# Two of 64 row maxima of a unit taken over by ScalarE, GpSimd and a short VectorE reduction

## The chip, the cores and the metric

The kernel runs on one core of one Trainium2 chip. The metric is the device time of one execution in microseconds (us); the time of record is the median of a few runs. TensorE (PE in the profile, PEld for its weight loads), VectorE (DVE), ScalarE (ACT), GpSimd (POOL) and SyncE (SP, which issues nearly all DMAs) each work through their own instructions in order and wait for each other by semaphores.

## What is computed

Two attention blocks share one input of 2048 tokens by 512, and a gate mixes their outputs. Cut to what matters here:

```python
x = A_x
g = sigmoid((x * gate_w).sum(-1, keepdims=True))
# A: 32 heads of 16, every query sees all 2048 keys
p = softmax(einsum("bhqd,bhkd->bhqk", q, k) * scale, axis=-1)
a = einsum("bhqk,bhkd->bhqd", p, v) ... @ A_wo
# B: 32 heads, four segments of 512 tokens; within a segment causal softmax,
# plus a memory term from the segments before
for s in range(4):
    p = softmax(einsum(qs, ks) * scale + mask)
    o = g_h * (pq @ M) / (pq @ z + 1e-6) + (1 - g_h) * (p @ vs)
    M, z = M + pk.T @ vs, z + pk.sum()
b = o ... @ B_wo
out = g * a + (1 - g) * b
```

The maximum of every row of scores is needed before the exponentials. The kernel gets it with a first pass of score products, on the orientation that has the queries on the partitions, and folds it into the second pass, on the transposed orientation, as two extra rows of q.

## The kernel before

A first stage (until about 300 us) computes q, k, v and the memory, and begins with the maxima. Then the main stage runs over 2368 slots. A unit is a side (A or B), four heads and one chunk of 512 queries; an A unit has 64 slots, a B unit 10, and they alternate, so 74 slots make a pair of units.

In slot n, three things are issued. The score product (`score_product`, L1064) puts a 128x512 tile `st` into one of three PSUM banks and ScalarE takes its exponential to `p` in SBUF (L1083). The max product (L242), for the slot that is `LEAD` = 96 slots ahead, puts a 128x512 tile into one of four PSUM banks `sm`, and VectorE reduces it to one column of `pm` (`max_part`, L275: a TENSOR_REDUCE over 512 columns). About every seventh max slot belongs to side B; there VectorE runs up to two masked reductions (L290). The score and the max product of a slot use different halves of TensorE's rows.

After every third slot (`BURST` = 3) comes a run of P @ V (`some_values`, L155): pieces of 128 queries of four heads, usually three or four pieces. `most(n)` sets how many; `MOST` = 3 is the short run. All P @ V of a unit accumulate in the one bank `ops`; when the unit is done ScalarE copies `ops` to `oraw` (L1137) and SP stores it.

Twelve slots in every pair of units are a stretch of their own (`unit_end`): no P @ V runs there, and 24 half products of the output projection (or of a later q tile) go through the same bank `ops`, between the score and max products of the twelve slots. It begins right after, or within a few slots after, the last P @ V of an A unit. The P @ V of the B unit follows it: its pieces come from three `p` tiles, the first read by the first run after the stretch, the second by the second half of the second run.

GpSimd serves four things in one queue. (1) The diagonal tiles of B's `p` are masked by AFFINE_SELECT (L1092, `score_values`): one select for the first tile, then three together, two for the second tile and one for the third. P @ V of a tile waits for its select. (2) When a unit's last maximum is there, `finish_max` (L214 to L224) joins the columns of `pm`; TensorE transposes them and a DMA places them in the q tile. (3) An octet of heads that is done is normalised (`octet`): the factors, with a power (L1200) first, and later the scaling of the 128x512 tile `v` (L1216), for B the memory's share `vM` added (L1218), then the two halves `hl` (L1224, L1225), which SP stores. (4) Halves of weights (L948, L949) and the sum of two output parts (L1307). `at(n, f)` puts an action into the program when slot n is reached; within the twelve-slot stretch such actions come between its steps.

Of the kernel before, what the change touches and what calls it, by code (L numbers as in the profile page):

```python
# [10 lines left out]
F32 = mybir.dt.float32  # L11
F32R = mybir.dt.float32r
AF = mybir.ActivationFunctionType
ALU = mybir.AluOpType
AX = mybir.AxisListType
# [7 lines left out]
CH = 512  # L23
# [11 lines left out]
LEAD = 96  # L35
BURST = 3
LATER = (2, 3)
MOST = 3
# [9 lines left out]
def gated_mix(ctx, tc, x, xT, wqkv, a_wo, b_wq, b_wk, b_wv, b_wo, beta, gate_w, out):  # L48
    nc = tc.nc
# [67 lines left out]
    maxs = []  # L117
    for k in range(NU):
        mine = {u: iter(range(32)) for u in range(2)}
# [13 lines left out]
    last_max = {u: m for m, (u, _) in enumerate(maxs)}  # L133
# [23 lines left out]
    def wait_early(n, count=BURST):  # L157

        loads_ = []
        for m in range(n + 1 + LEAD, n + 1 + count + LEAD):  # L160
            if m < nS:
                u, (r, i) = maxs[m]
                loads_ += lands.pop(("q", u, r), []) + lands.pop(("k", u, r, u[2] if u[0] == "B" else i // 8), [])
        for u, j in slots[n + 1:n + 1 + count]:
            for r in range(2):
                loads_ += lands.pop(("score", u, r), [])
        for x in loads_:
            tc.add_manual_dep(behind[0].ins, x.ins.name, mybir.DependencyInfo(
                mybir.DependencyClass.Sync, mybir.DependencyReason.DATA), reason="loads of the next burst")
# [71 lines left out]
    def max_product(ps, u, h, s, n0, n, k, k0=0):  # L241
        nc.tensor.matmul(ps[:, n0:n0 + n], rows(qt[u][:, :, s * 128:(s + 1) * 128], h, 48), rows(k[:, :, k0:k0 + n], h, 48),  # L242
                         start=True, stop=True)
# [3 lines left out]
    def flush_rows():  # L247
        while rows_left:
            rows_left.pop(0)()
# [3 lines left out]
    def oldest():  # L253

        return min(read_last, key=read_last.get)

    def was_read(b):

        if b is not None:
            read_last[b] = count[0] = count[0] + 1  # L260
    count = [4]

    def max_part(m, bank, b=None):

        u, (r, i) = maxs[m]
        side, g, c = u
        if u not in pmt:
            pmt[u] = mp.tile([128, 4, 4] + [4] * (side == "A"), F32, tag="pm" + side, name="pm")
        pm = pmt[u]
        ps = bank()  # L270
        if side == "A":

            kc, s, h = i // 8, i % 8 // 2, 2 * r + i % 2
            max_product(ps, u, h, s, 0, CH, kt_[u, kc])
            nc.vector.tensor_reduce(pm[:, h, s, kc:kc + 1], ps, axis=AX.X, op=ALU.max, negate=True)  # L275
            was_read(b)
            flush_rows()
        else:


            k = kt_[u, c]
            if b is not None:
                read_last[b] = 9 * nS
            mine = [(2 * r + h, s, 128 * (s == 2) + 256 * (s == 1 and h), 128 * (s + 1))
                    for h, s in (((0, 0), (0, 2)), ((0, 1), (1, 1)), ((1, 0), (1, 2)), ((0, 3),), ((1, 3),))[i]]
            for h, s, n0, w in mine:
                max_product(ps, u, h, s, n0, w, k)
            flush_rows()
            def masked(h, s, n0, w):
                nc.vector.tensor_tensor_reduce(  # L290
                    out=tri["rest"][:, 0:w], in0=ps[:, n0:n0 + w], in1=tri["mask"][:, CH - w:], scale=-1.0, scalar=3.0e38,
                    op0=ALU.add, op1=ALU.min, accum_out=pm[:, h, s:s + 1])
                was_read(b)

            for h, s, n0, w in mine:
                rows_left.append(lambda h=h, s=s, n0=n0, w=w: masked(h, s, n0, w))
            rows_left.pop(0)()
        if m == last_max[u]:
            def finish():

                due = min(e for e in a_last if e >= last_max[u]) + LATE_T
                late.append((min(due, first[u] + LEAD - 12), u, finish_max(u)))
            todo.append((m + 1, finish))
# [616 lines left out]
    fr = ctx.enter_context(tc.tile_pool(name="fr", bufs=1, reuse_waits="tile"))  # L920
# [4 lines left out]
    banks = [sm_ps.tile([128, CH], F32, name=f"sm{i}") for i in range(4)]  # L925
# [111 lines left out]
    wide = range(nS - LEAD + 2, nS - 4)  # L1037
# [6 lines left out]
    queue = []  # L1044
# [121 lines left out]
    def at(n, f):  # L1166
        beside.setdefault(n, []).append(f)
# [188 lines left out]
    def most(n):  # L1356

        if not queue:
            return 0
        _, u, done = queue[0]  # L1360
        side, left = u[0], SLOTS[u[0]] - done
        runs = (first[u] + SLOTS[side] + GAP[side] + 1 - n) // BURST
        if side == "B" or runs < 1:
            return ends[side].get(left, MOST + (len(queue) > LOW))
        due = min(SLOTS[side], (n + BURST - GAP[side] - first[u] + 1) // 4 * 4) - done
        return MOST + (left - 4 >= (MOST + 0.5) * runs and (due > 2 * MOST or runs == 1))
# [1 line left out]
    filled = [0]  # L1368
    turns = [0]

    def maximum(n):

        b = oldest()
        max_part(n + LEAD, lambda: banks[b], b)

    def unit_end(n0):

# [49 lines left out]
    n = 0  # L1427
    while n < nS or queue or beside or filled[0] < len(fill):
        for f in beside.pop(n, []):
            f()  # L1430
        if shared and n % BURST == 0:
            n += END - 1
            unit_end(n - END + 1)
            for x in range(n - END + 1, n + 1):
                for f in beside.pop(x, []):
                    f()
            wait_early(n)
            n += 1
            continue
        if n < nS:  # L1440
            score_tile(n)
            score_product(n)
            score_values(n)
        m = n + LEAD
        if m < nS:
            loads(m + PRE)
            maximum(n)
        run_todo(m)
        if n >= nS or n % (2 * BURST if n in wide else BURST) == (2 * BURST if n in wide else BURST) - 1:
            taken = some_values(n, 8 if n >= nS or n in wide else most(n))  # L1450
            if n < 5:


                for i in range(4):
                    nc.tensor.matmul(ops[:, 128 * i:128 * i + 128], identf, identf, start=True, stop=True)
            if any(e[0] < m + 1 for e in late):
                run_late(st_ps, "st", m + 1)
            else:

                for _ in range(0 if n >= nS and queue else 4 if n not in wide else 11 - taken if taken < 8 else 0):  # L1460
                    if filled[0] == len(fill) or fill[filled[0]][0] > n:
                        break
                    fill[filled[0]][1]()
                    filled[0] += 1
            if 5 < n < nS:
                wait_early(n)
        n += 1
# [3 lines left out]
    for b in range(4):  # L1471
# [3 lines left out]
        t = fr.tile([128, D], F32, tag="v" if b % 2 else "res", name="res", bufs=2)  # L1475
# [37 lines left out]
```

## Time and profile before

| what | value |
|---|---|
| median of 3 runs | 1750.01 us (1749.66 to 1750.13) |
| profiled execution, own time | 1750.37 us |
| its span in the trace | 1748.7 us |
| granted TensorE clock | 1.000 |
| busy, of the span: PE | 1730.6 us (99%) |
| DVE | 1599.5 us (91%) |
| ACT | 1439.9 us (82%) |
| POOL | 735.6 us (42%) |
| DMA | 261.67 MB, mean 150 GB/s |

The span runs from the first to the last recorded instruction; 1.7 us of the execution lie outside it. A row of a group gives the instructions' summed busy time, the mean of one, and the idle time of the engine just before them with what ended it. Records of neighbouring instructions overlap, so the step from one start to the next says more of an engine's rate than the mean length does. The ends of matmuls are modelled, so starts are used for TensorE as well.

### The profile page before, as it was taken

Reading aid. Unit: us, or ns where it says so; the run is one execution under the profiler, and the core shown is the slowest. Engines: PE = TensorE matmul, PEld = TensorE weight load, DVE = VectorE, ACT = ScalarE, POOL = GpSimd, SP = SyncE. Lnnn points to the kernel's source line nnn. Section 1 sums busy time; section 2 is a strip of 40 time slices with the busy share of each in tenths; the row PEclk is TensorE's granted clock in tenths of the full one; section 3 lists DMA queues with packets and bytes.
Section 4 is the critical chain, followed back from the end, with each engine's and each line's share of the span. In section 5 each row is a group of like instructions: output and inputs, shape, how many; then the busy total and the mean of one; then the engine's idle time right before and its main releaser. Section 6 shows DMA issues by size and latency. Waiting matters only on the chain.

```text
span 1748.7 us, 42288 instructions
## 1 busy us (share of the span) xinstructions
PE 1730.6 (99%) x15565; PEld 922.6 (53%) x15565; DVE 1599.5 (91%) x3327; ACT 1439.9 (82%) x2763; POOL 735.6 (42%) x992
## 2 busy tenths in 40 slices
PE   9999999999999999999999999999999999999999
PEld 7887775544444455444444444445444445444445
DVE  7757788999999999999999999999999999999931
ACT  6545557898888898888888888888888888888884
POOL 3543233234352427443435253535344353435442
PEclk9999999999999999999999999999999999999999
DMA  6786567335443446454545454455445444544542
GB/s 207 259 287 218 197 226 213 116 100 147 123 150 106 138 121 182 127 148 124 142 132 147 121 149 124 133 145 127 143 130 148 128 131 118 150 118 145 149 152 63
DMA packets 149390, 261.67 MB, mean 150 GB/s; under 512 B 39064, under 2 KB 61624, under 8 KB 148672
## 3 DMA queue, kind: packets, MB, share of 16 engines
q1 hardware_dynamic: 146640, 254.42, 48.8%
q0 software_dynamic: 2400, 4.29, 0.9%
q8 instruction: 124, 2.03, 0.5%
q14 instruction: 82, 0.67, 0.1%
q10 hardware_dynamic: 144, 0.26, 0.1%
HBM read 174.39 MB, written 83.25 MB: 147 GB/s over the span
## 4 chain that ended last, share of the span: by engine, by line
PE 97%; ACT 2%; issue 0%; DMA 0%; DVE 0%; POOL 0%
PE ops L155 39%; PE st L1064 27%; PE sm L242 14%; PE pr L366 9%; PE pair L366 4%; PE sm L155 2%; ACT p L1083 1%; PE mt_ps L232 0%; PE tps L831 0%; PE sm L1064 0%; DMA vs<-wqkv 0%; PE mps L845 0%; ACT res L1305 0%; PE num L804 0%; PE den L808 0%
## 5 line engine op out<-in xcount | busy, mean ns | idle before, releaser
L1083 ACT ACTIVATE p<-st 128x512 f32<-128x512 f32 x2261 | 1196.2, 603 | 150.2 <-PE sm L242 97.8
L275 DVE TENSOR_REDUCE pm<-sm 128x1 f32<-128x512 f32 x2048 | 1279.7, 683 | 11.2 <-PE sm L242 8.8
L242 PE MATMUL sm<-kA,qA 48*128 48x512 f32 x2048 | 688.3, 428 | 0.1
L1064 PE MATMUL st<-qA,kA 50*128 50x512 f32 x2014 | 676.9, 430 | 7.7 <-ACT p L1083 7.2
L1064 PEld LDWEIGHTS st<-qA,kA 50*128 50x128 f32 x2014 | 332.1, 185 | 419.1 <-ACT p L1083 382.5
L155 PE MATMUL ops<-p,vA 128*17 128x256 f32 (+3 forms) x6360 | 552.2, 445 | 0.0
L242 PEld LDWEIGHTS sm<-kA,qA 48*128 48x128 f32 x2048 | 339.8, 185 | 14.6 <-DVE ph L449 3.9
L1200 POOL TENSOR_TENSOR rcp<-rec,minus 128x32 f32<-128x32 f32 x43 | 234.8, 5461 | 89.3 <-DMA rec<-dend 85.0
L290 DVE CUSTOM_DVE_ANT_0 rest<-sm,mask 128x128 f32<-128x128 f32 (+3 forms) x512 | 246.8, 482 | 0.2
L155 PEld LDWEIGHTS ops<-p,vA 128*17 128x17 f32 x6360 | 129.3, 96 | 214.3 <-issue 183.7
L1092 POOL TENSOR_SCALAR_AFFINE_SELECT p<-p 128x512 f32<-128x512 f32 x128 | 78.6, 637 | 289.9 <-ACT p L1083 288.5
L242 PE MATMUL sm<-kB,qB 48*128 48x128 f32 (+3 forms) x512 | 162.7, 378 | 0.0
L1064 PE MATMUL st<-qB,kB 50*128 50x512 f32 (+2 forms) x495 | 114.2, 329 | 0.3 <-ACT mt L235 0.3
L1064 PEld LDWEIGHTS st<-qB,kB 50*128 50x128 f32 x495 | 77.7, 186 | 47.2 <-ACT p L1083 35.2
L155 PE MATMUL ops<-p,vB 128*17 128x128 f32 (+3 forms) x1504 | 87.5, 350 | 0.0
L155 PE MATMUL ops<-wA,blk 64*128 64x512 f32 x264 | 78.9, 405 | 3.1
L242 PEld LDWEIGHTS sm<-kB,qB 48*128 48x128 f32 x512 | 80.3, 185 | 0.2
L214 POOL TENSOR_TENSOR dm<-pm 128x32 f32<-128x32 f32 x32 | 7.9, 247 | 170.0 <-DVE pm L275 170.0
L155 PE MATMUL ops<-wB,blk 64*128 64x512 f32 x264 | 75.5, 392 | 0.0
L437 POOL TENSOR_SCALAR mn<-full 128x512 f32<-128x512 f32 x24 | 37.0, 1540 | 76.9 <-ACT full L432 76.9
L223 POOL CAST ms<-pm 128x16 fp32r<-128x16 f32 x32 | 6.3, 197 | 136.4 <-DVE pm L290 136.4
L155 PEld LDWEIGHTS ops<-wA,blk 64*128 64x128 f32 x264 | 45.5, 185 | 14.8 <-issue 11.6
(319 smaller groups left out, 1752.3 us busy)
## 6 DMA issues: line engine op xcount, KB each, us to landing
kA<-kdA SPq DMA_DIRECT2D x256, 128.0 KB
vA<-vdA SPq DMA_DIRECT2D x31, 544.0 KB
kA<-kdA SPq DMA_DIRECT2D x256, 64.0 KB
qB<-qdB SPq DMA_DIRECT2D x192, 64.0 KB
kB<-kdB SPq DMA_DIRECT2D x192, 64.0 KB
kdA<-q SPq DMA_DIRECT2D x32, 256.0 KB
qdB<-q SPq DMA_DIRECT2D x32, 256.0 KB
qA<-qdA SPq DMA_DIRECT2D x64, 128.0 KB
```

The source lines that it names most:

```text
L155: behind[0] = nc.tensor.matmul(*args, **kw)
L214: nc.gpsimd.tensor_sub(dm, pm[:, :, :, 2:4], pm[:, :, :, 0:2])
L223: nc.gpsimd.tensor_copy(ms[:, :, 0], nv)
L242: nc.tensor.matmul(ps[:, n0:n0 + n], rows(qt[u][:, :, s * 128:(s + 1) * 128], h, 48), rows(k[:, :, k0:k0 + n], h, 48), start=True, stop=True)
L275: nc.vector.tensor_reduce(pm[:, h, s, kc:kc + 1], ps, axis=AX.X, op=ALU.max, negate=True)
L290: nc.vector.tensor_tensor_reduce(out=tri["rest"][:, 0:w], in0=ps[:, n0:n0 + w], in1=tri["mask"][:, CH - w:], scale=-1.0, scalar=3.0e38, op ...
L366: nc.tensor.matmul(ps, l, r, start=start, stop=stop)
L437: nc.gpsimd.tensor_scalar_min(ph["mn"], full, 0.0)
L1064: nc.tensor.matmul(ps[:, n0:n0 + CH - q0], rows(k[:, :, b * 128:(b + 1) * 128], h, 50), rows(q[:, :, q0:], h, 50), start=True, stop=True)
L1083: nc.scalar.activation(p[:, h], ps, AF.Exp, scale=SCALE)
L1092: nc.gpsimd.affine_select(out=x, in_=x, pattern=[[0, 4], [1, 128]], base=0, channel_multiplier=-1, compare_op=ALU.is_ge, fill=0.0)
L1200: eng.tensor_tensor(r, rec, minus, op=ALU.pow)
```

## The change

In `maximum`, for the last slot of a burst, the length of the P @ V run that follows is looked at. If it is over three pieces, and the max slot belongs to an A unit with more than 40 max slots left, and the unit has given away fewer than two (`SHARE`) and none in the last 20 slots (`SPACE`), then VectorE doesn't reduce the bank. ScalarE copies the 128x512 bank to SBUF (`halves`). Two, four and six slots later GpSimd halves it to 256, 128 and 64 columns; a halving is three instructions, a difference, a clamp and a sum, which together make the larger of two values. Thirty-four slots after the copy VectorE reduces the 64 columns that are left. Slots of `unit_end` and of the last 96 slots never do this. In this program 50 of 2048 A maxima are moved, the first at slot 59 and the last at slot 2213, one or two a unit.

```diff
-    def max_part(m, bank, b=None):
+    def max_part(m, bank, b=None, copied=None):
...
-            nc.vector.tensor_reduce(pm[:, h, s, kc:kc + 1], ps, axis=AX.X, op=ALU.max, negate=True)
+            if copied:
+                copied(ps, pm[:, h, s, kc:kc + 1])
+            else:
+                nc.vector.tensor_reduce(pm[:, h, s, kc:kc + 1], ps, axis=AX.X, op=ALU.max, negate=True)
...
-    def maximum(n):
+    SHARE, SPACE = 2, 20
+    taken_by = {}
+
+    def by_halves(n):
+
+        def copied(ps, pm):
+            t = fr.tile([128, CH], F32, tag="halves", name="halves", bufs=2)
+            nc.scalar.copy(t, ps)
+
+            x = fr.tile([128, CH // 2], F32, tag="above", name="above", bufs=1)
+
+            def halve(w):
+                nc.gpsimd.tensor_sub(x[:, 0:w], t[:, 0:w], t[:, w:2 * w])
+                nc.gpsimd.tensor_scalar(x[:, 0:w], x[:, 0:w], 3.0e38, 0.0, op0=ALU.min, op1=ALU.max)
+                nc.gpsimd.tensor_add(t[:, 0:w], t[:, w:2 * w], x[:, 0:w])
+            for i, w in enumerate((256, 128, 64)):
+                at(n + 2 + 2 * i, lambda w=w: halve(w))
+            at(n + 34, lambda: nc.vector.tensor_reduce(pm, t[:, 0:64], axis=AX.X, op=ALU.max, negate=True))
+        return copied
+
+    def maximum(n, run=0):
 
         b = oldest()
-        max_part(n + LEAD, lambda: banks[b], b)
+        u = maxs[n + LEAD][0]
+        mine = taken_by.setdefault(u, [])
+        yes = (run > MOST and u[0] == "A" and len(mine) < SHARE and last_max[u] - n - LEAD > 40
+               and not (mine and n - mine[-1] < SPACE))
+        if yes:
+            mine.append(n)
+        max_part(n + LEAD, lambda: banks[b], b, by_halves(n) if yes else None)
+
+    def next_run(n):
+
+        return min(most(n), sum(e[0] <= n and e[1] == queue[0][1] for e in queue)) if queue else 0
...
-            maximum(n)
+            maximum(n, next_run(n) if n % BURST == BURST - 1 and n not in wide else 0)
```

TensorE's and SP's instructions stand in the same order before and after. Three places show what moves elsewhere; line numbers differ by 3 or 33 between the two programs.

On GpSimd, the twelve-slot stretch that begins at slot 1104 (about 957 us in the trace of before). `p` is the tile that the select masks for P @ V, `v`, `vM` and `hl` are the scaling of an octet. Before, from the first select to the three selects for the second and third tile:

```order
L1092 AFFINE_SELECT p<-p 128x4x128
L1216 TENSOR_TENSOR v<-v,inv 128x512
L1218 TENSOR_TENSOR v<-v,vM 128x512
L1224 CAST hl<-v 128x4x128
L1225 TENSOR_TENSOR hl<-v,hl 128x4x128
L1092 AFFINE_SELECT p<-p 128x4x128 x3
```

And now, from the third instruction of the first halving on (the first select and the other two of that halving stand directly ahead of it):

```order
L1388 TENSOR_TENSOR halves<-halves,above 128x256
L1386 TENSOR_TENSOR above<-halves 128x128
L1387 TENSOR_SCALAR above<-above 128x128
L1388 TENSOR_TENSOR halves<-halves,above 128x128
L1386 TENSOR_TENSOR above<-halves 128x64
L1387 TENSOR_SCALAR above<-above 128x64
L1388 TENSOR_TENSOR halves<-halves,above 128x64
L1219 TENSOR_TENSOR v<-v,inv 128x512
L1221 TENSOR_TENSOR v<-v,vM 128x512
L1227 CAST hl<-v 128x4x128
L1228 TENSOR_TENSOR hl<-v,hl 128x4x128
L1095 AFFINE_SELECT p<-p 128x4x128 x3
```

The nine instructions of slot 1103's maximum now stand between the first select and the scaling, and so ahead of the three selects.

On the same engine, the stretch that begins at slot 1251 (about 1047 us), where two moved maxima, those of slots 1226 and 1247, come close together. Before, from the last factor of an octet on:

```order
L1206 TENSOR_TENSOR rec<-rec,gB_3261 128x32
L1092 AFFINE_SELECT p<-p 128x4x128
L1216 TENSOR_TENSOR v<-v,inv 128x512
L1218 TENSOR_TENSOR v<-v,vM 128x512
L1224 CAST hl<-v 128x4x128
L1225 TENSOR_TENSOR hl<-v,hl 128x4x128
L1092 AFFINE_SELECT p<-p 128x4x128 x3
```

Now, from the last three instructions of slot 1247's second halving on; ahead of them, behind the factor, stand the nine of slot 1226 and the three of slot 1247's first halving:

```order
L1386 TENSOR_TENSOR above<-halves 128x128
L1387 TENSOR_SCALAR above<-above 128x128
L1388 TENSOR_TENSOR halves<-halves,above 128x128
L1095 AFFINE_SELECT p<-p 128x4x128
L1386 TENSOR_TENSOR above<-halves 128x64
L1387 TENSOR_SCALAR above<-above 128x64
L1388 TENSOR_TENSOR halves<-halves,above 128x64
L1219 TENSOR_TENSOR v<-v,inv 128x512
L1221 TENSOR_TENSOR v<-v,vM 128x512
L1227 CAST hl<-v 128x4x128
L1228 TENSOR_TENSOR hl<-v,hl 128x4x128
L1095 AFFINE_SELECT p<-p 128x4x128 x3
```

Fifteen instructions now stand between the factor and the first select, and three more between that select and the scaling.

On ScalarE, the end of the A unit at slot 881 (about 820 us). `p<-st` are exponentials, `oraw<-ops` empties the bank that the stretch at slot 882 uses next. Before:

```order
L235 CAST mt<-mt_ps 64x128
L1083 ACTIVATE p<-st 128x512 x15
L1137 COPY oraw<-ops 128x512
L1083 ACTIVATE p<-st 128x512 x3
L1080 ACTIVATE p<-st 128x2x256
```

Now:

```order
L235 CAST mt<-mt_ps 64x128
L1086 ACTIVATE p<-st 128x512 x15
L1381 COPY halves<-sm_3294 128x512
L1140 COPY oraw<-ops 128x512
L1086 ACTIVATE p<-st 128x512 x3
L1083 ACTIVATE p<-st 128x2x256
```

The copy of a maximum stands directly ahead of the copy of `ops`, with no exponential between them.

## The prediction

> **What bounds the kernel now.** I read the window of the main stage first, then the timeline of TensorE and VectorE inside it, then the waits. The columns of the first row are the window, its length, and busy time with instruction counts of PE, PEld, DVE, ACT and POOL.
>
> ```profile
> 320.00:1660.00 1340.00, 1328.16 (x12905) 645.80 (x12905) 1337.42 (x2851) 1195.48 (x2308) 574.17 (x784) 1.00 0.47 134
> ```
>
> Two engines look full: VectorE with 1337 of 1340 us and TensorE with 1328. Which of them waits for the other decides what 50 removed reductions are worth. Two stretches of VectorE and one of TensorE say it.
>
> ```profile
> 802.60 7.86 DVE L275 TENSOR_REDUCE pm<-sm 128x1 f32<-128x512 f32 x13
> ...
> 842.59 7.62 DVE L275 TENSOR_REDUCE pm<-sm 128x1 f32<-128x512 f32 x12
> ```
>
> ```profile
> 803.47 0.84 PE L155 MATMUL ops<-p,vA 128*17 128x384 f32 x8
> 804.24 0.50 PE L1064 MATMUL st<-qA,kA 50*128 50x512 f32 x1
> ...
> 805.17 1.05 PE L155 MATMUL ops<-p,vA 128*17 128x512 f32 x8
> 806.15 0.50 PE L1064 MATMUL st<-qA,kA 50*128 50x512 f32 x1
> ```
>
> A reduction is 0.683 long. The first stretch steps (7.86 - 0.68)/12 = 0.598 us, the second (7.62 - 0.68)/11 = 0.631. So 0.598 is VectorE's own rate, three of them 1.79 us a burst, and in the second stretch it loses 0.1 us a burst although no idle shows. TensorE's burst with a run of four pieces is 804.24 to 806.15 = 1.91 us, 0.93 for the products and 805.17 to 806.15 = 0.98 for the run; a run of three takes 803.47 to 804.24 = 0.77, which makes 1.70. Where runs are of four, TensorE is the slower one and VectorE waits for it. TensorE in its turn hardly waits for VectorE:
>
> ```profile
> PEld sm L242 <- DVE pm L275: 0.3, 2, 0.2
> PEld ops L155 <- POOL p L1092: 1.2, 5, 0.2
> ```
>
> The columns are us in total, times and longest. That list counts idle weight loads alone, so I looked for places where a product starts just when its bank is released. One is the end of a twelve-slot stretch:
>
> ```profile
> 918.24 0.69 DVE L275 TENSOR_REDUCE pm<-sm 128x1 f32<-128x512 f32 x1
> ...
> 918.65 0.18 PEld L1064 LDWEIGHTS st<-qA,kA 50*128 50x128 f32 x1 [0.34 <-ACT p L1083]
> ...
> 918.98 0.18 PEld L242 LDWEIGHTS sm<-kA,qA 48*128 48x128 f32 x1
> ```
>
> The max product should start with the score product at 918.65 and starts at 918.98, 0.05 after the reduction ends at 918.93: 0.33 us lost to VectorE. In short: TensorE sets the pace, VectorE trails by one or two per cent, and what delays TensorE, from whichever engine, goes into the time in full.
>
> **VectorE, removed and added.** Removed are 50 x 0.598 = 29.9 us. Added are 50 reductions of 64 columns from SBUF, which no row shows. The nearest are the masked reductions, here with a 384- and a 128-column tile:
>
> ```profile
> L290 DVE CUSTOM_DVE_ANT_0 rest<-sm,mask 128x384 f32<-128x384 f32 x120 | 65.7, 548 | 0.0
> ...
> L290 DVE CUSTOM_DVE_ANT_0 rest<-sm,mask 128x128 f32<-128x128 f32 x120 | 33.8, 281 | 0.1
> ```
>
> The slope is (548 - 281)/256 = 1.04 ns a column, so 0.598 - 448 x 0.00104 = 0.13 us; the bounds are 0.07 (the slope alone) and 0.28. I take 0.13. VectorE is relieved by 50 x 0.47 = 23.4 us, but only what lasts until a place like 918.98 reaches TensorE. The relief is lost wherever VectorE waits for TensorE before that, as in the stretch of fours. Ahead of 918.98 one maximum is taken at slot 1025, four bursts before; I count 0.2 us of the 0.33 as won there, since the short reduction of an earlier maximum comes back in between, and five such places among the 50: -1.0 us, with -7 as the far end (0.46 us at fifteen places).
>
> **ScalarE, added.** Each copy is like the copy of `ops`, which steps 821.42 - 820.94 = 0.48 us:
>
> ```profile
> 820.94 0.59 ACT L1137 COPY oraw<-ops 128x512 f32<-128x512 f32 x1
> ...
> 821.42 1.09 ACT L1083 ACTIVATE p<-st 128x512 f32<-128x512 f32 x2
> ```
>
> Fifty make 24 us. In a burst of 1.91 us the three exponentials take some 1.45 (three of about 0.48), so the copy ends near the moment the next exponential is due, and three score banks cover the rest. That cover is missing where the copy stands directly ahead of `oraw` (slot 881): the last exponential ends just before 820.94 now, so `oraw` starts 0.4 later, and so does the first half product, which needs the emptied bank and follows `oraw` closely now. Ten takes stand so. In five the stretch ends at a place like 918.98, where TensorE then arrives later and loses less to VectorE; I count these at nothing and the other five at 0.4 each: +2.0 us (0 to 4).
>
> **GpSimd, added.** Nine instructions a maximum. Their prices come from these groups (x count | busy, mean ns | idle before):
>
> ```profile
> L1216 POOL TENSOR_TENSOR v<-v,inv 128x512 f32<-128x512 f32 x31 | 39.8, 1284 | 26.0 <-DMA inv<-rdA 19.7 <-DMA inv<-rdB 4.9 <-DMA qB<-qdB 1.3
> L437 POOL TENSOR_SCALAR mn<-full 128x512 f32<-128x512 f32 x24 | 37.0, 1540 | 76.9 <-ACT full L432 76.9
> ...
> L1224 POOL CAST hl<-v 128x512 fp32r<-128x512 f32 x31 | 18.9, 610 | 2.0
> ```
>
> ```profile
> 805.75 0.24 POOL L214 TENSOR_TENSOR dm<-pm 128x32 f32<-128x32 f32 x1 [7.43 <-DVE pm L275]
> 806.07 0.31 POOL L215 TENSOR_SCALAR dm<-dm 128x32 f32<-128x32 f32 x1
> ```
>
> Between 32 and 512 columns a two-input operation costs 0.24 to 1.28 us, so 0.73, 0.45 and 0.31 at 256, 128 and 64; a one-input operation, by L215 and L437, 0.31 to 1.54, so 0.88, 0.56 and 0.39. That is 2 x 1.49 + 1.83 = 4.8. Between dependent instructions lies 806.07 - 805.75 - 0.24 = 0.08, nine times 0.7: 5.5 us a maximum, 275 us in all. If the clamp ran at the rate of the CAST (0.61 at 512) it would be 4.8; with two operations in the clamp, and no row for minimum and maximum together, twice the clamp is the other bound, 7.3. [...]
>
> GpSimd is 43% busy and most of its work has microseconds to spare: the copies at slots 857, 935 and 1004 find it idle, and VectorE's short reduction comes 34 slots later. What matters is what stands behind the nine. In the stretch at slot 1104 that is an octet's scaling and then the selects for P @ V of side B:
>
> ```profile
> 956.88 0.65 POOL L1092 TENSOR_SCALAR_AFFINE_SELECT p<-p 128x512 f32<-128x512 f32 x1 [5.56 <-ACT p L1083]
> 957.59 1.28 POOL L1216 TENSOR_TENSOR v<-v,inv 128x512 f32<-128x512 f32 x1
> ...
> 962.25 1.80 POOL L1092 TENSOR_SCALAR_AFFINE_SELECT p<-p 128x512 f32<-128x512 f32 x3
> ```
>
> ```profile
> 966.63 0.84 PE L155 MATMUL ops<-p,vB 128*17 128x128 f32 x16
> ```
>
> The second half of the run at 966.63 needs the second tile's first select. A run grows by 0.98 - 0.77 = 0.21 us a piece, so that half starts at about 966.87. Before, the select was done at 962.25 + 0.64 = 962.9, 4 us early. Now: free at 957.5, nine instructions until 963.0, scaling 962.25 - 957.59 = 4.66 until 967.7, select until 968.3, and the wait takes 0.05: 1.5 us late. TensorE stands in order, so everything behind the piece waits too. Four takes are like this one (slots 659, 1103, 1547, 1991; a fifth, 215, has a shorter scaling behind it and just about fits): +6.0 us.
>
> In the stretch at slot 1251 two maxima are queued:
>
> ```profile
> 1041.90 0.25 POOL L1206 TENSOR_TENSOR rec<-rec,gB 128x32 f32<-128x32 f32 x1
> ...
> 1053.44 1.81 POOL L1092 TENSOR_SCALAR_AFFINE_SELECT p<-p 128x512 f32<-128x512 f32 x3
> ```
>
> ```profile
> 1057.22 0.84 PE L155 MATMUL ops<-p,vB 128*17 128x128 f32 x16
> ```
>
> From 1042.2: two maxima 11.0 and the first select 0.65, so the scaling starts at 1053.8, takes 4.66, and the select, which was done at 1054.1, is done at 1059.1; the piece is due at 1057.46: 1.7 us late. Five takes are like this (slots 359, 803, 1247, 1691, 2135): +8.5 us. At 4.8 us a maximum the two kinds give 0.8 and 0.3 (5 us in all), at 7.3 they give 3.3 and 5.3 (40 us). I keep 5.5.
>
> **The sum.** Profiled execution 1750.4, VectorE -1.0, ScalarE +2.0, GpSimd +6.0 + 8.5: **1765.9 us**. The profiled execution is 0.4 above the median of the runs, less than I can resolve.
>
> **Rivals.** (1) VectorE is the bound after all. For it: 1337 of 1340 us. [...] Then the relief of 50 x 0.47 counts in full: 1750.4 - 23.4 = 1727, or 1743 if only the waits like 918.98 go (-7) and GpSimd is in time. It decides if TensorE's bursts shorten when VectorE is ahead; against it stands that VectorE's step grows to 0.631 where runs are of four. Chance 0.13. (2) Nothing to be measured: TensorE bounds and GpSimd's halvings cost less than 4.6 us, so the selects are in time. 1750.4 - 1.0 + 2.0 = 1751. Chance 0.15. (3) ScalarE becomes the bound: each of 50 copies delays the next exponential and with it TensorE by 0.4, +20 us: 1770, with GpSimd's part 1784. Against it: ScalarE is busy 1195 of 1340, and 24 us more fit. Chance 0.08. That the change doesn't do what it says is ruled out by the order, which has 50 copies.
>
> **Chances and range.** The forecast has 0.64. What a measurement here can tell from no change is about 0.2%, 3.5 us. Faster 0.13 from rival 1; same 0.15 from rival 2; slower 0.72 from the forecast and rival 3. The range takes in rival 2 and the lower price of the clamp (1756) and reaches to 1780, which is 6.3 us a maximum (2.3 and 3.3 us at the two kinds); rival 1 and the far end of the costs stay out: 1748 to 1780.
>
> **What would show it.** Right: in the list of waits, P @ V (L155) waits for the select (L1095) by about 1.5 us at nine places, the first selects after the scaling come 4 to 5 us later than now relative to TensorE, the nine GpSimd instructions sum to 5.5 us, and VectorE shows idle time while TensorE's bursts keep 1.7 and 1.9. Wrong: no wait for GpSimd above 0.5 us; TensorE's bursts shorter than 1.6 us; a clamp of 256 columns at 0.4 us; or a shift of the start of every burst after a copy.

## The result, and the profile after

The kernel after takes 1761.22 us (median of 4 runs, 1760.62 to 1762.15) against 1750.00 (1749.66 to 1750.13): 11.2 us slower, ratio 1.0065 with a 95% interval of 1.0047 to 1.0082. The span of the profiled execution grew from 1748.7 to 1760.4, by 11.7 us. Of the four executions, two had a mean granted TensorE clock of 0.999 and took 1762.15 (the profiled one) and 1761.78 us, and two had 1.000 and took 1760.67 and 1760.62; the last section comes back to this. The forecast was 1765.9 in a range of 1748 to 1780.

First the window of the main stage, the same view as before (window, length, then busy time and count of PE, PEld, DVE, ACT and POOL):

```profile
320.00:1672.00 1352.00, 1334.58 (x12909) 643.42 (x12913) 1324.13 (x2850) 1213.97 (x2357) 768.26 (x1233) 1.00 0.46 133
```

VectorE was busy for 1337 of 1340 us and is now for 1324 of 1352. Its relief has turned into idle time, and the list of waits says what it waits for (us in total, times, longest):

```profile
DVE pm L278 <- PE sm L242: 19.6, 43, 5.0
PEld ops L155 <- ACT oraw L1140: 14.7, 40, 0.4
PEld ops L155 <- POOL p L1095: 4.9, 7, 2.1
PE ops L155 <- POOL p L1095: 3.1, 2, 1.8
PE ops L155 <- ACT oraw L1140: 1.8, 9, 0.2
```

VectorE waits for max products, so for TensorE. TensorE has two kinds of new waits, and neither was in the list of before at this size, which had these two rows in their place:

```profile
PEld ops L155 <- ACT oraw L1137: 10.5, 30, 0.4
PEld ops L155 <- POOL p L1092: 1.8, 7, 0.3
```

So ten weight loads more wait for `oraw`, 0.42 us each. They are the ten of the copies that stand directly ahead of the copy of `ops`. ScalarE at slot 881, after, to be held against the rows from 820.94 on of before:

```profile
828.23 0.61 ACT L1381 COPY halves<-sm 128x512 f32<-128x512 f32 x1
828.69 0.63 ACT L1140 COPY oraw<-ops 128x512 f32<-128x512 f32 x1
```

TensorE there, before and after: the last score product, then the first half product of the stretch, which needs the emptied bank `ops`.

```profile
821.40 0.40 PE L1064 MATMUL st<-qB,kB 50*128 50x384 f32 x2
821.64 0.43 PE L155 MATMUL ops<-wA,blk 64*128 64x512 f32 x1
```

```profile
828.76 0.40 PE L1067 MATMUL st<-qB,kB 50*128 50x384 f32 x2
829.38 0.49 PE L155 MATMUL ops<-wA,blk 64*128 64x512 f32 x1 [0.21 <-ACT oraw L1140]
```

The distance was 821.64 - 821.40 = 0.24 and is 829.38 - 828.76 = 0.62: 0.38 us lost, while the row itself shows a wait of 0.21 only, since the product before it still runs.

The two long waits for a select are at slots 359 (1.33 us) and 659. The second:

```profile
700.75 1.00 PE L155 MATMUL ops<-p,vB 128*17 128x256 f32 x8 [1.81 <-POOL p L1095]
```

GpSimd just ahead of it shows why this stretch is late and the one at slot 1104 is not. Here a halving of weights (`wA`) stands in the queue as well:

```profile
690.40 0.73 POOL L1386 TENSOR_TENSOR above<-halves 128x256 f32<-128x256 f32 x1
...
692.39 0.61 POOL L951 CAST wA<-wraw 128x512 fp32r<-128x512 f32 x1
693.08 1.29 POOL L952 TENSOR_TENSOR wA<-wraw,wA 128x512 fp32r<-128x512 f32 x1
694.32 0.46 POOL L1386 TENSOR_TENSOR above<-halves 128x128 f32<-128x128 f32 x1
...
696.80 1.29 POOL L1219 TENSOR_TENSOR v<-v,inv 128x512 f32<-128x512 f32 x1
...
700.05 1.81 POOL L1095 TENSOR_SCALAR_AFFINE_SELECT p<-p 128x512 f32<-128x512 f32 x3
```

The stretch at slot 1104 has the nine instructions and the scaling, but no weights:

```profile
965.58 0.72 POOL L1386 TENSOR_TENSOR above<-halves 128x256 f32<-128x256 f32 x1
...
970.16 1.29 POOL L1219 TENSOR_TENSOR v<-v,inv 128x512 f32<-128x512 f32 x1
...
974.81 1.81 POOL L1095 TENSOR_SCALAR_AFFINE_SELECT p<-p 128x512 f32<-128x512 f32 x3
```

From 965.58 to 970.16 is one maximum with all its gaps (the last instruction overlaps the scaling by a few hundredths): 4.6 us, where the prediction had 5.5. The groups give the prices (count | busy us, mean ns | idle before):

```profile
L1386 POOL TENSOR_TENSOR above<-halves 128x256 f32<-128x256 f32 x50 | 36.6, 732 | 38.0 <-ACT halves L1381 37.7
L1387 POOL TENSOR_SCALAR above<-above 128x256 f32<-128x256 f32 x50 | 20.0, 400 | 4.4
L1387 POOL TENSOR_SCALAR above<-above 128x128 f32<-128x128 f32 x50 | 14.7, 295 | 4.4
L1387 POOL TENSOR_SCALAR above<-above 128x64 f32<-128x64 f32 x50 | 12.0, 240 | 4.4
L1391 DVE TENSOR_REDUCE pm<-halves 128x1 f32<-128x64 f32 x50 | 10.4, 208 | 0.0
```

The two-input operations came out as foreseen (0.73 at 256), the clamp did not: 0.40, 0.30 and 0.24 instead of 0.88, 0.56 and 0.39.

At slot 359 the weights cost a second time, ahead of the select: a half product of the stretch itself waits for them.

```profile
507.53 0.50 PE L155 MATMUL ops<-wB,wA 64*128 64x512 f32 x1 [0.33 <-POOL wB L952]
```

TensorE's order is the same in both programs, so the two traces can be laid side by side slot by slot, by the start of each slot's score product. The difference of the starts grows by 11.7 us over the main stage, and most of that comes at places that can be named (a place's part is the growth from the slot of its take, that is of its moved maximum, to the slot of the next take):

| place | growth, us |
|---|---|
| ten takes directly ahead of `oraw` (slots 215, 437, ... 2213), nine of 0.35 to 0.45 and a last one of 0.2 | 3.8 |
| slot 359: 0.6 at the half products, 1.5 at the select | 2.1 |
| slot 659, without its 0.4 above | 3.4 |
| the other 39 takes, 0.06 each on the mean | 2.4 |
| together | 11.7 |

At slots 1103, 1547 and 1991, which have the nine instructions ahead of the scaling but no weights, nothing stays beyond the 0.4 of the first row: TensorE falls 0.1 us behind at the select and makes it up within a burst.

### The profile page after: what moved, and what is told of

Same layout as the page of the kernel before. It is cut to its first block, busy times and chain, and to the rows that moved or that the text cites. A ratio compares the mean times of both kernels' runs of the same rounds, so it can differ in the third digit from the quotient of the medians.

```text
span 1760.4 us, 42814 instructions
## 1 busy us (share of the span) xinstructions
PE 1736.4 (99%) x15565; PEld 919.4 (52%) x15565; DVE 1585.5 (90%) x3327; ACT 1458.7 (83%) x2813; POOL 929.6 (53%) x1442
## 4 chain that ended last, share of the span: by engine, by line
PE 91%; POOL 3%; ACT 3%; DVE 2%; issue 1%; DMA 0%; POOLq 0%; ACTq 0%; DVEq 0%
PE ops L155 36%; PE st L1067 24%; PE sm L242 13%; PE pr L369 9%; PE pair L369 4%; PE sm L155 2%; ACT p L1086 2%; DVE pm L278 1%; POOL rcp L1203 1%; PE mt_ps L232 0%; POOL halves L1388 0%; PE tps L834 0%; POOL above L1386 0%; PE sm L1067 0%; ACT oraw L1140 0%
## 5 line engine op out<-in xcount | busy, mean ns | idle before, releaser
L278 DVE TENSOR_REDUCE pm<-sm 128x1 f32<-128x512 f32 x1998 | 1252.3, 682 | 24.5 <-PE sm L242 19.6
L1386 POOL TENSOR_TENSOR above<-halves 128x256 f32<-128x256 f32 x150 | 75.7, 504 | 44.9 <-ACT halves L1381 37.7
L1388 POOL TENSOR_TENSOR halves<-halves,above 128x256 f32<-128x256 f32 x150 | 75.7, 504 | 12.5
L440 POOL TENSOR_SCALAR mn<-full 128x512 f32<-128x512 f32 x24 | 36.7, 1530 | 78.0 <-ACT full L435 78.0
```

What stands on the lines that cost most here:

```text
L440: nc.gpsimd.tensor_scalar_min(ph["mn"], full, 0.0)
L1386: nc.gpsimd.tensor_sub(x[:, 0:w], t[:, 0:w], t[:, w:2 * w])
L1388: nc.gpsimd.tensor_add(t[:, 0:w], t[:, w:2 * w], x[:, 0:w])
```

## The experiments

The theory at this point: TensorE sets the pace; ScalarE's copies cost something where TensorE waits for `oraw`; GpSimd costs where its halvings stand ahead of selects; VectorE's relief is worth nothing. The rivals: the relief is worth its 23 us and the costs are that much greater; or the work as such costs (contention), wherever it stands. All runs below are compared with the kernel before on the same chip, which had 1750.2 to 1750.4 us in all of them.

### VectorE's relief alone

```diff
-            t = fr.tile([128, CH], F32, tag="halves", name="halves", bufs=2)
-            nc.scalar.copy(t, ps)
...
-            for i, w in enumerate((256, 128, 64)):
-                at(n + 2 + 2 * i, lambda w=w: halve(w))
-            at(n + 34, lambda: nc.vector.tensor_reduce(pm, t[:, 0:64], axis=AX.X, op=ALU.max, negate=True))
+            nc.vector.tensor_reduce(pm, ps[:, 0:64], axis=AX.X, op=ALU.max, negate=True)
```

> VectorE's relief alone: for the 50 moved maxima VectorE reduces just the first 64 columns of the bank, at once; the other 448 columns are left out of these maxima, and there is no copy and no halving. Theory (TensorE sets the pace): 1749 to 1750 us, no difference that can be measured. Rival 1 (VectorE bounds): 50 x 0.47 less, 1727 us; or 1743 us if only the short waits for VectorE at the ends of the twelve-slot stretches go.

Measured: 1750.40 us, ratio 1.0000 (0.9991 to 1.0009). VectorE's relief of some 23 us changes nothing. In the slots' starts no take leaves a gain over 0.1 us, and all together leave 0.0. That settles the first rival of the prediction.

### The ceiling of such a relief

```diff
-        yes = (run > MOST and u[0] == "A" and len(mine) < SHARE and last_max[u] - n - LEAD > 40
-               and not (mine and n - mine[-1] < SPACE))
+        yes = (run > 0 and u[0] == "A")
```

with the edit of the run before.

> The ceiling of any relief of VectorE: 636 maxima of A (the last slot of nearly every burst that has a run behind it) are reduced over their first 64 columns alone, the other 448 columns are left out; no copy, no halving. VectorE is relieved by up to 636 x 0.47 = 299 us. Theory (TensorE sets the pace and loses to VectorE only in short waits such as 0.33 us at the ends of the twelve-slot stretches, some 15 such places): 1743 to 1749 us, with VectorE idle for some 300 us of the main stage. Rival 1 (VectorE bounds): at least as low as 1727 us, and down to where TensorE has no more slack: its busy time in the main stage, 1328 of 1340 us, so 1727 to 1738 us.

Measured: 1746.15 us, ratio 0.9976 (0.9966 to 0.9985), 4.2 us less for some 300 us of relief. Window (from 320 to 1660) and waits:

```profile
320.00:1660.00 1340.00, 1328.04 (x12920) 640.09 (x12916) 1105.44 (x2856) 1195.77 (x2310) 577.51 (x790) 1.00 0.46 135
```

```profile
DVE pm L278 <- PE sm L242: 140.9, 350, 5.0
DVE rest L293 <- PE sm L242: 95.3, 246, 0.6
```

VectorE is busy for 1105 us of 1340 and waits 236 us for products; TensorE is as busy as before, 1328 us. By the slots' starts, 2.1 us of the gain fall in the first 50 slots (280 to 310 us), 0.12 a burst. There the runs have three pieces, and a burst of 1.70 us is shorter than three reductions (1.79 us). In the rest of the main stage all the relief together wins under 2 us.

### The copies alone, VectorE as before

```diff
             nc.scalar.copy(t, ps)
...
-            for i, w in enumerate((256, 128, 64)):
-                at(n + 2 + 2 * i, lambda w=w: halve(w))
-            at(n + 34, lambda: nc.vector.tensor_reduce(pm, t[:, 0:64], axis=AX.X, op=ALU.max, negate=True))
+            nc.vector.tensor_reduce(pm, ps, axis=AX.X, op=ALU.max, negate=True)
```

> The 50 copies by ScalarE alone: the copies are made, nothing reads them, VectorE reduces all banks as before, GpSimd has nothing to do. Theory (TensorE sets the pace, ScalarE costs only where its copy stands directly ahead of the copy of `ops`): ten places of 0.42 us, so 1750.0 + 4.2 = 1754.2 us, up to 1756 if the small drift of the changed kernel (1.8 us that no place explains) is ScalarE's too. Rival 1 (VectorE's relief is worth its 23 us and something eats it, the copies being the only other change on every one of the 50 places): here the relief is gone and the copies remain, so clearly above the changed kernel, 1765 us or more. Rival 2 (ScalarE costs nothing, all 11 us are GpSimd's): 1750 us.

Measured: 1775.61 us, ratio 1.0144 (1.0130 to 1.0158). By the number this is the first rival's; the trace says something else. The program makes the two readers of a bank wait for each other, so each of the 50 reductions starts only when its copy is done:

```profile
DVE pm L1383 <- ACT halves L1381: 23.2, 50, 0.7
PEld sm L242 <- DVE pm L278: 12.6, 49, 0.5
```

VectorE waits 23.2 us for ScalarE, and TensorE then waits for VectorE at 49 places, where it hardly did before. From each take to the next, the slots' starts grow by 0.41 to 0.68 us (at the one of slot 59 by 0.11). So this run doesn't price the copies. What it shows is that 0.47 us less work at 50 places is worth nothing to the kernel, while a delay of VectorE of 0.46 us (23.2/50) at the same places goes into the time in full: VectorE is already as late as it may be. At the 40 takes that aren't directly ahead of `oraw` the growth is 20.7 us together; the copies themselves are 2.3 of it by the next run, and the 18.4 that are left stand against 40 x 0.46 = 18.6 us of delay.

### Copies and short reductions, without GpSimd

```diff
             nc.scalar.copy(t, ps)
...
-            for i, w in enumerate((256, 128, 64)):
-                at(n + 2 + 2 * i, lambda w=w: halve(w))
             at(n + 34, lambda: nc.vector.tensor_reduce(pm, t[:, 0:64], axis=AX.X, op=ALU.max, negate=True))
```

> The changed kernel without GpSimd's part: ScalarE copies the 50 banks, VectorE reduces 64 columns of the copy 34 slots later, no halvings (448 columns of these maxima are left out). In the run of the copies alone the 25 us came with VectorE's reductions starting only after the copy (50 waits, 23.2 us), so that run could not price ScalarE; this one can. Theory (ScalarE costs only directly ahead of the copy of `ops`): 1750.4 + 10 x 0.42 = 1754.6 us, up to 1756.2 if the drift is ScalarE's. Rival (each of the 50 copies delays TensorE by some 0.4 us, as the run of the copies alone would have it without VectorE's wait): 1770 us.

Measured: 1755.70 us, ratio 1.0032 (1.0019 to 1.0044), 5.5 us over the kernel before; 6.0 us in the slots' starts. The ten takes ahead of `oraw` make 3.8 of it. The other 40 copies have 2.3 us together, 0.06 each; at slots 116, 338, 413 and 560, for instance, it comes in one step, with the run of P @ V behind the second burst after the take. So the upper end of the theory held, and the 0.4 us a copy of the rival did not.

### GpSimd's work alone

```diff
-            t = fr.tile([128, CH], F32, tag="halves", name="halves", bufs=2)
-            nc.scalar.copy(t, ps)
+            t = own()
...
-            at(n + 34, lambda: nc.vector.tensor_reduce(pm, t[:, 0:64], axis=AX.X, op=ALU.max, negate=True))
+            nc.vector.tensor_reduce(pm, ps, axis=AX.X, op=ALU.max, negate=True)
```

where `own()` gives one tile of zeros.

> GpSimd's work alone: the nine instructions of each of the 50 maxima stand where they stand in the changed kernel, on one tile of zeros, their result is not used; no copy, and VectorE reduces all banks as before. Theory (GpSimd costs only where its halvings stand ahead of the selects behind the halving of weights, at slots 359 and 659): +5.6 us, 1755.6 us, with waits of P @ V for the select of 1 to 2 us at these two places and none elsewhere. Rival 1 (GpSimd and VectorE get in each other's way, 50 x 4.65 us of halvings slow VectorE's reductions): above 1758 us, with reductions longer than 0.683 us while GpSimd halves. Rival 2 (all of the change's 11 us are GpSimd's): 1761 us.

Measured: 1756.23 us, ratio 1.0036 (1.0024 to 1.0049), 5.85 us over the kernel before. The size is the theory's, the places not quite:

```profile
PE ops L155 <- POOL p L1095: 4.5, 5, 2.2
```

Five waits instead of two: beside slots 359 (1.30 us) and 659 (2.19 us) the stretches of slots 1103, 1547 and 1991, with 0.55 us each in the slots' starts, of which 0.4 stay. In the kernel after, TensorE itself comes 0.4 us later to these three, because of the copy ahead of `oraw`, and so loses 0.1 there instead, of which nothing stays. VectorE's reductions keep their 683 ns, so they are not slowed by GpSimd's work. The two parts, 6.0 and 5.7 us in the slots' starts, add up to the 11.7 of the kernel after, but not place by place: GpSimd's work alone costs 1.2 us more at these three and 1.2 us less at slot 659 (2.2 against 3.4; the last section has the clock there).

### The halvings later in the queue

```diff
-                at(n + 2 + 2 * i, lambda w=w: halve(w))
+                at(n + 14 + 2 * i, lambda w=w: halve(w))
```

> The changed kernel with the halvings 14, 16 and 18 slots after the copy instead of 2, 4 and 6, so that those of slots 659, 1103, 1547 and 1991 stand behind the scaling and the three selects. Theory: GpSimd's lateness is a matter of the place in its queue alone; 1761.2 - 5.8 = 1755.4 us, with no wait of P @ V for a select above 0.5 us there. Rival (what costs is GpSimd's work as such, by contention with VectorE or TensorE): 1761 us as before the move.

Measured: 1756.71 us, ratio 1.0038 (1.0026 to 1.0051), 4.5 us less than the kernel after by the medians, and the waits for a select are back at the size of before:

```profile
PEld ops L155 <- POOL p L1095: 1.3, 5, 0.3
```

The same work in another place of the queue costs TensorE little: 6.4 us are left in the slots' starts, of which 6.0 are the copies'.

### No take directly ahead of `oraw`

```diff
-               and not (mine and n - mine[-1] < SPACE))
+               and not (mine and n - mine[-1] < SPACE) and n % 222 != 215)
```

> The changed kernel without the ten takes that stand directly ahead of the copy of `ops` (slots 215, 437, ... 2213); 40 remain. Theory: ten waits of TensorE for `oraw` go (4.2 us by the slots' starts) and with them the halvings behind slots 659, 1103, 1547 and 1991 (another 2.7 us): 1754.3 us; what is left is the stretch of slot 359 (2.2 us) and the drift. Rival (the cost is spread evenly over the 50 copies): four fifths of 11 us, 1759 us.

Measured: 1754.38 us, ratio 1.0024 (1.0015 to 1.0034), where 1754.3 was expected. The weight loads that wait for `oraw` are 30 again, as before the change:

```profile
PEld ops L155 <- ACT oraw L1140: 10.5, 30, 0.4
PE ops L155 <- POOL p L1095: 1.3, 1, 1.3
```

The one long wait for a select that is left is slot 359's.

### Both repairs

This kernel has the edits of the last two runs together.

> Both repairs at once: no take directly ahead of the copy of `ops` (40 takes remain) and the halvings 14, 16 and 18 slots after the copy. Theory: neither the waits for `oraw` nor those for a select are left; what stays is 0.05 us a copy, two bursts after it, 40 x 0.05 = 2 us: 1752.2 us, and nothing is gained, since VectorE's relief is worth nothing in the main stage. Rival 1 (the relief shows once nothing is in its way): below 1749 us. Rival 2 (the cost goes with the number of copies and halvings, not with their places): 1755 to 1759 us.

Measured: 1752.39 us, ratio 1.0011 (1.0002 to 1.0020), where 1752.2 was expected. With all waits gone that could be named, 40 reliefs of VectorE still win nothing, and 40 copies still cost 2 us (2.3 in the slots' starts).

### The clamp twice

```diff
                 nc.gpsimd.tensor_scalar(x[:, 0:w], x[:, 0:w], 3.0e38, 0.0, op0=ALU.min, op1=ALU.max)
+                nc.gpsimd.tensor_scalar(x[:, 0:w], x[:, 0:w], 3.0e38, 0.0, op0=ALU.min, op1=ALU.max)
```

> The changed kernel with each clamp made twice (the second changes nothing): 0.40 + 0.30 + 0.24 and three gaps of 0.08 more, 1.18 us a maximum, so 5.8 instead of 4.65 us, a little over the 5.5 us of the prediction. Theory (the prediction's places were right and only its price was too high): the first kind of place later by 1.2 us, four of them, and the second kind, which is just in time at 4.65, by 2.4 us, five of them: 4.7 + 12 = 16.5 us above the changed kernel, 1774 to 1778 us, with waits for a select at all nine places. Rival (the places themselves were wrong and only the two stretches with the halving of weights stall): 1.2 to 2.4 us more at each of these two, 1764 to 1766 us.

Measured: 1784.80 us, ratio 1.0199 (1.0185 to 1.0213), more than the theory's 1778. Eight of the nine places of the prediction now show: TensorE waits for the select at the second half of the second run, for instance in the stretch of slot 1103. At the ninth, slot 359, it waits for halved weights instead.

```profile
PE ops L155 <- POOL p L1095: 16.0, 8, 4.3
```

```profile
990.65 0.63 PE L155 MATMUL ops<-p,vB 128*17 128x256 f32 x8 [1.36 <-POOL p L1095]
```

In the slots' starts the three of the first kind without weights grow by 1.6 us each at this wait and the four of the second kind without weights by 2.1. With 5.83 us a maximum the prediction's own sum gives 1.5 + 0.33 = 1.8 and 1.7 + 0.66 = 2.4, and at the first kind TensorE itself is 0.4 late. What goes beyond the theory lies at slots 359 (7.2 us) and 659 (6.9 without the 0.4), and there the granted clock is the news. The window behind slot 359 (the column after POOL's is the clock):

```profile
512.38:526.03 13.65, 13.15 (x70) 7.49 (x66) 8.46 (x18) 7.62 (x15) 11.62 (x21) 0.50 0.10 40
```

For 13.65 us TensorE had half its clock, and for 6.83 us more behind slot 659. In this run the half products of a stretch start every 0.23 us at the full clock (508.35 to 509.28) and every 0.43 at half of it (515.16 to 516.87), so the half clock is up to 10.2 us of the time, half of 20.48, an estimate.

### Where VectorE does bound: four and three early maxima

```diff
-        yes = (run > MOST and u[0] == "A" and len(mine) < SHARE and last_max[u] - n - LEAD > 40
-               and not (mine and n - mine[-1] < SPACE))
+        yes = (u[0] == "A" and n in (2, 11, 20, 29))
...
-            at(n + 34, lambda: nc.vector.tensor_reduce(pm, t[:, 0:64], axis=AX.X, op=ALU.max, negate=True))
+            at(n + 12, lambda: nc.vector.tensor_reduce(pm, t[:, 0:64], axis=AX.X, op=ALU.max, negate=True))
```

> The changed kernel's way for four maxima only, at slots 2, 11, 20 and 29, with the short reduction 12 slots after the copy, and none of the 50 others. With 636 maxima relieved, 2.1 us of the 4.2 us gained came in the first 50 slots (0.12 us a burst), where all runs have three pieces and TensorE's burst (1.70) is shorter than three reductions (1.79 to 1.81). Theory (there, and there alone, VectorE bounds): 4 x 0.47 = 1.9 us less, 1748.3 us, down to 1749 if the copies and GpSimd's queue take a part. Rival (the gain there had another cause, or the copies eat it): 1750 us.

Measured: 1753.39 us, ratio 1.0018 (1.0010 to 1.0027), neither theory's. By slot 36 TensorE was 0.8 us ahead of the kernel before. Then the short reduction came before GpSimd was done, since halvings of weights stood in its queue, and VectorE stood still, with all other maxima behind it:

```profile
302.83 0.22 DVE L1391 TENSOR_REDUCE pm<-halves 128x1 f32<-128x64 f32 x1 [2.44 <-POOL halves L1388]
```

That wait is the smaller part of the loss. TensorE lost 1.8 us by slot 37, standing idle for 1.07 us up to 303.71, and 3.7 more by slot 45, for from there on it had half its clock for 10.24 us:

```profile
303.72:313.96 10.24, 10.24 (x61) 4.90 (x63) 7.59 (x14) 4.46 (x9) 9.01 (x23) 0.50 0.60 191
```

The next run has three takes (slots 2, 11 and 20) and reduces at slots 15, 26 and 40, behind the halvings' end.

> Three maxima only, at slots 2, 11 and 20, with their short reductions at slots 15, 26 and 40, after GpSimd has long finished the halvings; none of the 50 others. In the run with four such maxima TensorE was 0.8 us ahead of the kernel before by slot 36, then VectorE waited 2.44 us for the halvings of slot 20 at its short reduction and all was lost. Theory (VectorE bounds in the first 50 slots alone): up to 3 x 0.47 = 1.4 us less, 1749 us, too little to tell from 1750.3 for certain, but to be seen in the slots' starts. Rival (GpSimd's later halving of weights costs more than that): above 1751 us.

Measured: 1750.56 us, ratio 1.0001 (0.9992 to 1.0010). The slots' starts show 0.8 us won by slot 36, 0.1 lost again at slot 45 and 0.7 at slot 51. There TensorE waits to transpose the maxima of a finished unit, which GpSimd joins (`ms`); its eight instructions for that stand behind a halving of weights, which starts at 307.23 instead of 304.42, when its weights have landed:

```profile
311.67 0.41 PE L232 MATMUL mt_ps<-identf,ms 128*32 128x128 f32 x2 [0.27 <-POOL ms L224]
```

So the gain of the first 36 slots is real, and the late halving of weights in GpSimd's queue eats it: the cause that the rival named, at less than its cost. Why those weights land later was not followed. No version of this idea was found that beats the kernel before by an amount that can be measured, and the ceiling run says that there are 4 us at the most.

## Why the prediction was right, point by point

The direction and the bound held, and so did the kinds of wait that cost; the two large terms were mis-sized in opposite directions, most of GpSimd's cost came from what the prediction does not have, and the range was wide enough for what was left.

**What bounds.** Right. The reading of VectorE's step (0.598 us where runs are of three, 0.631 where they are of four) told more than its 1337 of 1340 us busy: relieved by some 23 us it won 0.0 us, by some 300 us 4.2. What the prediction did not say is the other half: VectorE has no slack. In the run of the copies alone, 18.6 us of delay at 40 places cost 18.4.

**VectorE, -1.0.** It measured 0 (ratio 1.0000). The 0.2 us at places like 918.98 did not come, because the prediction misread that place. In the run of the relief alone VectorE arrives there early, stands idle for 0.19 us until TensorE's product is done, and the next max product still comes 0.33 us behind its score product:

```profile
917.95 0.69 DVE L278 TENSOR_REDUCE pm<-sm 128x1 f32<-128x512 f32 x1 [0.19 <-PE ops L155]
918.36 0.18 PEld L1067 LDWEIGHTS st<-qA,kA 50*128 50x128 f32 x1 [0.46 <-ACT p L1086]
918.69 0.18 PEld L242 LDWEIGHTS sm<-kA,qA 48*128 48x128 f32 x1
```

What holds the max product there is one reduction that starts as soon as TensorE's own product is done and ends at 918.64, not VectorE's lateness, and an earlier relief did not shorten it. The price of the short reduction, 0.13, was right: in the kernel after one starts at 694.56 and the next reduction at 694.68.

```profile
694.56 0.21 DVE L1391 TENSOR_REDUCE pm<-halves 128x1 f32<-128x64 f32 x1
694.68 0.68 DVE L278 TENSOR_REDUCE pm<-sm 128x1 f32<-128x512 f32 x1
```

**ScalarE, +2.0.** It measured 6.0 in the slots' starts (5.5 by the medians), 3.8 ahead of `oraw` and 2.3 elsewhere. The mechanism ahead of `oraw` was right, with 0.42 for 0.4. Two parts of the step failed: "I count these at nothing" for five of the ten, on the ground that TensorE would lose less to VectorE at the stretch's end, which no stretch shows; and the three score banks, which cover the other 40 copies almost, but not quite: 0.06 us each. Which instruction TensorE waits for there can't be read from the rows, so that the score banks are the cause is only argued.

**GpSimd, +6.0 and +8.5.** It measured 5.7. The step that failed first is the choice of L437 as the row for the clamp: the clamp took 0.40, 0.295 and 0.24 us at 256, 128 and 64 columns, and by the slope of the first two, 0.105 us for 128 columns, it would take 0.61 at 512 (an estimate), as much as the CAST does (0.61). The prediction's other price, by the rate of the CAST, 4.8 us a maximum, is nearer to the measured 4.6 than its 5.5. Why the one-input operation of the first stage (now L440) takes 1.53 us at 512 columns was not tried and stays open.

With the right price the prediction's mechanism holds where it can be seen alone: at 4.65 us a maximum its sum leaves 1.5 - 0.85 = 0.65 at the first kind, measured 0.55 with GpSimd alone, and 1.7 - 1.7 = 0 at the second kind, measured 0; with two clamps its places wait, eight of nine. But it adds two terms that overlap: its four takes of the first kind are among the ten ahead of `oraw`, where TensorE itself comes 0.4 later. In the kernel after, seven of the nine places cost nothing that stays. The 5.7 us come almost whole from the two others, 2.1 at slot 359 and 3.4 at slot 659, where weights are halved in the same queue, and 1.5 of the 3.4 are TensorE's halved clock. The prediction has neither. That the sum for the cheaper clamp, 5 us for the two kinds, lies near 5.7 is luck as well, since it has them at nine places.

**Its own signs.** Of the signs of being right, VectorE's idle time came, but the waits of about 1.5 us at nine places were two, of 1.3 and 1.8, and a maximum took 4.6 us, not 5.5. Of the signs of being wrong, a clamp of 0.4 us at 256 columns came exactly, and a shift behind the copies came at 0.06 us. They tell against the size of the GpSimd term and, weakly, against the cover of the score banks; the bound they leave standing.

**The sum.** 0 + 6.0 + 5.7 = 11.7 against a forecast of -1.0 + 2.0 + 14.5 = 15.5. The errors of +1, +4 and -9 met in part. The reasons carried the direction; the nearness of 1765.9 to 1761.2 is largely luck.

## What to carry to other kernels

An engine that is busy for 99.8% of the time may be following another: compare its own fastest step with its step in the stretches where the other's burst is longer, and take work away from it in a trial run that simply leaves the work out, before building a path that moves it elsewhere. Where two engines run in step, as here, relief of the follower can be worth nothing (0.0 us for 23) and a delay of it can cost in full (18.4 us for 18.6). Work moved to an engine with idle time is priced by what stands behind it in that engine's queue at each place (here 5.7 us ahead of the selects and 0.4 twelve slots later), and the places where other rare work (here halvings of weights) is in the same queue come first.

## What the hardware showed that was not expected

A short wait of TensorE (1.81 us at slot 659) can be followed by half its clock. In the traces here the clock is halved behind such a wait for 3.41 us or two, three or four times that (6.83 and 13.65 in the run of two clamps, 10.24 in that of four early maxima). In the trace of the kernel after the clock changes at 700.86, 704.27 and, with TensorE's work done, 1758.99: the last two lie 1054.72 us apart, 309 stretches of 3.413. The windows below are stretches of that length, in line with the changes of their trace. The kernel after around slot 659, where the wait of 1.81 us ends at 700.75 (busy time and count of PE, PEld, DVE, ACT and POOL, then the clock):

```profile
697.44:700.86 3.42, 1.61 (x22) 0.77 (x22) 2.98 (x5) 2.13 (x5) 3.27 (x5) 1.00 0.14 44
700.86:704.27 3.41, 3.41 (x34) 1.68 (x33) 1.73 (x4) 1.57 (x3) 3.33 (x5) 0.50 0.38 154
```

The place lost 3.4 us in the slots' starts, 1.6 more than the wait itself. From the start of the run behind the wait (700.75) to the score product behind the next run (704.72) it takes 3.97 us; the same work at the full clock, with GpSimd's work alone, takes 2.44 (699.02 to 701.46), so 1.5 of the 1.6 are the half clock. The two executions of this kernel with a clock of 1.000 were 1.3 us shorter on the mean than the two with 0.999, so the halving does not seem to come every time. With GpSimd's work alone the same place waited longer, kept its clock in the profiled execution, and lost 2.2. There the wait lies across two stretches, 0.98 us of idle time in the first and 1.21 in the second:

```profile
699.02 0.63 PE L155 MATMUL ops<-p,vB 128*17 128x256 f32 x8 [2.19 <-POOL p L1095]
...
694.39:697.80 3.41, 2.44 (x24) 0.88 (x23) 3.41 (x8) 3.07 (x7) 3.11 (x5) 1.00 0.45 153
697.80:701.21 3.41, 2.19 (x38) 1.19 (x38) 1.58 (x4) 1.04 (x3) 3.33 (x6) 1.00 0.38 154
```

So the length of the wait alone doesn't tell what the clock does. The idle time within one stretch doesn't either. In the run of two clamps 1.54 us of idle time in one stretch did not halve the clock, while 1.12 us did, with a longest wait of 0.80 at 511.90 (13.65 us at half clock followed), as did the 1.07 us of the four early maxima:

```profile
1635.36:1638.77 3.41, 1.87 (x30) 1.03 (x34) 1.54 (x5) 1.24 (x3) 2.67 (x4) 1.00 0.38 154
508.96:512.38 3.42, 2.30 (x18) 1.17 (x14) 2.49 (x6) 1.83 (x4) 3.34 (x4) 1.00 0.49 153
```

What else counts, and what ends the half clock, stays open.

A wait of 1.81 us was followed by half the clock here and one of 2.19 was not in another run. A stall of TensorE can therefore cost more than its own length (3.4 us for 1.81), and a sum of waits alone is then too low.
